# Gated linear attention into a gMLP: a pair of chunks first, decays as one exponential, fewer shifts, another order table

## Chip, cores and metric

The kernel runs on one core of one Trainium2 chip. Its time is device microseconds of one execution. Before the change the median of three runs is 139.16 us (138.14, 139.16 and 139.8).

The engines are named as in the profile: PE (TensorE, matmuls), PEld (its weight loads), DVE (VectorE), ACT (ScalarE), POOL (GpSimd) and SP (SyncE), whose queue issues all large loads and stores.

## The reference

Two parts follow each other. The first is a recurrence with a decay for each token, head and state row; the second is a gated MLP that mixes along the sequence.

```python
for t in range(S):                                   # B, H, S, D = 4, 8, 768, 48
    state = alpha[:, :, t, :, None] * state + np.einsum('bhd,bhe->bhde', k[:, :, t], v[:, :, t])
    y[:, :, t] = np.einsum('bhd,bhde->bhe', q[:, :, t], state)
...
h = np.maximum(x @ w_in, 0.0)                        # x: 4 x 768 x 384, w_in: 384 x 1024
u, v = (h[..., :512], h[..., 512:])
v_n = (v - mean(v)) / np.sqrt(var(v) + 1e-06)
v_s = np.einsum('ts,bsd->btd', w_spatial, v_n) + b_spatial[None, :, None]
return (u * v_s) @ w_out
```

## The kernel before, in words

A batch of 768 tokens is six chunks of 128, so there are 24 chunks, numbered i, and 12 pairs of chunks, numbered j = i // 2. For each chunk the kernel takes the logarithm of alpha (op `ln`), sums it along the tokens with a triangular matmul (`cum`, `half`), and takes exp(-sum) and exp(sum) on ACT (`einv`, `eexp`). The keys are multiplied by the first (`kt`), the queries by the second (`qt`); both are transposed on PE (`tr`, `trk`) and copied back (`ev`, `evs`). Scores (`sc`) are masked on DVE (`m`, `ms`), multiplied by the values and added to the part from the old state (`ya`, `y`), and the result is copied into xT (`xe`). `upd` makes the chunk's k'v, `z` adds the old state, and `S` multiplies by the decay over the chunk, exp of the total sum, which `ebc` puts into a small tile; `sb` copies the state to bf16.

Chunks are handled in three ways. A quad (`four_chunks`, line 653) loads four chunks at four tokens a partition, in runs of 768 bytes; a pair (`pair`, line 428) loads two at two tokens a partition, in runs of 384 bytes; a single (`single`, line 870) loads one chunk in runs of 192 bytes. Lines 92 to 94 say which j are which: a quad starts at j = 0 (chunks 0 to 3 of batch 0) and at j = 3 (batch 1), a pair is j = 2 (chunks 4 and 5), and all the rest are singles. A plain pair or quad (j = 0, 2) sums its tokens by matmul alone, the other multiplies neighbouring alphas first (`pr`). Each of alpha, k, q and v is one DMA for a quad, a pair or a single chunk, into one of three rotating buffers.

The decay: the totals are small matmuls with `la` as weights and `ones_col`, `halves_of` or `quarters_of` as the moving operand (lines 471, 700, 901), one column for a head pair and chunk. Each column holds two heads, one in each half of the partitions, and `ebc` (lines 501, 723, 913) takes the exponential of each half by itself into its column of a tile `bc` or `bcq`, whose other half must stay zero so that heads do not mix. That is two activations for each pair, quad or single, and the tiles are zeroed at the start (lines 296 and 316).

The MLP: `v` and `u` are products of xT with the halves of w_in, `ve` and `ue` their relus. `bn` takes the statistics of v on DVE (lines 1067, 1068), `rs` makes 1/std on ACT (Ln, Exp; lines 1077, 1078), `nm` (line 1082) makes the shift -mean/std of two token tiles on DVE, and `vn` normalises, on DVE from mean and 1/std (line 1096) or on ACT from 1/std and the shift (line 1092). `s` mixes along the sequence, `se` adds the bias, `g` gates, `o` is the last product, `oe` evicts it and `st` stores it.

What runs where and when is written out in a table, PLAN (lines 42 to 88). A word such as `P62@0:512#0` says: engine PE, op number 62, PSUM bank 0, and ahead of it a filler matmul of 512 columns on bank 0 (`warm`, line 239, fp32, issued as two records). `replay` (line 109) emits the ops in that order, so each engine's own order is the table's, and each engine takes its instructions strictly in that order. The letters also choose the engine where an op may run on several: evictions and relus on ACT or DVE, key products on POOL or DVE, casts on POOL, ACT or DVE.

At the start, the table loads the quad (four loads of 768 KB), then the first half of w_in that `v` needs, then the pair, batch 1's quad, the second half of w_in and w_spatial between them. POOL builds the masks and triangles; `causal` (line 350), the pair's mask, stands on POOL between two key products of the quad.

Of the kernel before, what the change touches and what calls it, by code (L numbers as in the profile page):

```python
# [21 lines left out]
class Op:  # L22


    def __init__(self, key, engs, emit, deps, take, pe):
        self.key, self.engs, self.emit, self.take, self.pe = key, engs, emit, take, pe
        self.deps = [d for d in deps if d is not None]
        self.done = False


class Slot:
# [11 lines left out]
D2 D0 D4 D1 G9 G11 G5 G6 D3 S56 S57 S59 S58 A60 S12 S169 S170 A61 S275 S171 D8 P62@0:512#0:512#0:512#0 P66@1 P67 P63  # L43
P70@2 P71 P74@3 P75 A68 A64 D79 G82 P91@4,5 P52@6 A69 A72 A76 G7 A78 A92 A84 A65 G88 G87 A73 A77 D85 D90 D81 D93 D53
D83 D80 P103@6,4,5,7:512#7:424#7 P94@0,1 D86 D104 D89 D106 G13 P97@6,2:192#2 D98 A95 P100@3,0 D101 A96 P117@3,6:376#1
P115@4,1 A99 G107 G14 A15 A173 D102 D109 P128@0,2 D119 D118 P174@5 A116 A122 A176 P130@6,4 S16 D132 D131 S172 A135
P175@1 A129 P120@3 P54@2 G110 G105 P136@0,4 A121 A178 A55 G111 G108 P133@6 G181 A180 A134 G184 A179 D112 A177 D138
P123@7,3 P141@2 S20 G279 G280 G281 G17 G19 G18 D124 D125 P151@6 P187@7,4 P126@3 S23 S277 S276 D185 A152 A127 G186 G183
G113 G114 D182 P190@5,6 A189 A192 A142 P144@3 D137 P139@4 D188 D191 A140 G22 G21 D153 D143 P199@6,5 P196@2,7 P162@4
A283 A145 P290@0 A163 P154@1 P160@3 A282 A291 A155 D200 D201 D198 D197 D164 P193@4 A161 P156@7 A157 A165 D194 D146  # L50
P158@5 A159 G195 P202@1,2 P203 S26 A204 A147 D166 P293@4 P37@5,7 D38 P34@3,6 G24 S278 S387 S399 G25 S506 S29 D35
P207@1 D148 D208 D36 A39 A292 P205 P284@7 P40@3,5 A206 A285 A167 G10 D42 P210@2 D149 D150 D41 S388 S389 D168 D209 S401
S400 P287@5 P223@6 P219@3 P221@1 A211 A294 A224 A288 D212 A286 A220 A213 D298 D304 A289 A295 D214 D222 D215 A216
P225@6 P233@2 P217@3 P229@7 P237@0 A218 A28 D301 G300 G27 D307 G297 P226 D227 G303 G306 P43@3,5 D45 P230 P234 D231
D235 A296 A44 P46@4,6 P309@5,1 D311 P238 P49@7,3 D50 D51 A48 A47 A310 P312@2,6 P318@1,4 P315@5,7 P249@3 P250 A313 A319
A317 A299 A314 A302 D316 D320 D239 G236 D251 P341@4,1 P335@7,5 P245@0 P246 G305 G308 D336 D342 G232 P321@7,6,3,2 G240
G228 D343 D322 A510 G33 D337 D324 D247 P253@4 P333@7,1 P254 P241@5 P242 G323 A391 A403 A30 A340 A334 A32 G325 P392@0
D255 P348@7,6 D243 D327 D350 A393 P344@4 A394 P338@5 G31 G328 D397 D330 D349 G396 P404@3 A345 A339 A405 A406 P257@1
A395 S495 S390 A258 P260@4 P359@2 S402 G407 G248 G326 G329 S494 S560 P346@0,7 D408 P354@3,5 P410@1,6 A360 D331 A347
A353 A411 D356 D355 P362@2 G252 G398 P351@7 A352 P357@3 D412 S508 S497 S509 P421@6,1 P416@5,0 D361 S496 S507 S562 S550  # L60
S548 S611 S561 S551 S549 A358 A363 D418 D423 P511@7 P369@3 P413@0 P374@2 P380@1 D414 D417 A261 A512 P378@0 D422 A498
D364 A375 A564 P263@5 P499@6 G244 G332 G409 G256 A370 A379 A513 D371 G415 A500 A501 P419@0 P424@3 A425 G517 G505 G503
D381 D382 D516 G515 A420 P266@2 P269@4 A502 A365 A383 A270 D366 D504 P429@0 P426@1 P438@3 P440@6 D384 A368 A430 A427
P436@4 A437 A441 A385 D264 D439 P272@0 D367 D267 D428 D431 D386 P521@1 P372@4 A514 A273 P565@6 P376@2 A377 A432 A552
P442@7 A568 P529@0 D443 D522 P456@3 D433 D434 A435 A566 A567 D373 P452@7 P553@1 P518@2,5 A519 A554 A556 D520 A555 P457
D458 D530 D570 G569 G523 G557 G459 P444@4 P445 P448@5 D446 P453 D454 P468@6 P449 D558 D450 P533@7,4 P524@2,0 P572@1,3
D525 G451 G455 P472@5 P469 P460@2 P473 D526 D534 D535 G531 G447 D474 S623 A559 P575@7 D576 A573 P461 S625 S612 S563
A615 D470 D462 P616@4 P527@5 P536@1 A627 S613 A574 P579@7,3 P588@6,0 G577 A617 A528 D589 A618 A537 P628@5 A629 A571
G475 P538@2 A630 P464@1 S624 S614 S730 S718 S721 S626 S720 G620 D621 D581 D580 S733 S732 P476@6 G631 G578 P541@3
P584@7 A539 A619 A542 P465 S784 S719 A477 D632 P634@5,4 D590 A636 D466 D585 S731 A722 P591@3 S786 S772 S785 S773 S835  # L70
S774 A592 S787 S775 G622 G532 P582@1 A583 D635 D540 P637@7 P482@6 A633 A483 P723@5 G586 G471 D638 G639 A724 P645@3,4
P640@0,2 D543 G463 G587 P479@7 P604@6 P596@1 D646 D642 D641 A734 A726 D647 G729 G467 A605 A741 G727 P593@3 P600@6 A594
# [16 lines left out]

PAIRS = (2,)
QUADS = (0,3)
PLAIN = (0, 2)
IDLE = 16

SPLIT = ()
SMALL = ()


SUMS = (
# [30 lines left out]
def kernel(  # L132
# [134 lines left out]
    def op(key, engs, emit, deps=(), take=(), use=(), pe=None):  # L267
# [3 lines left out]
        for s in list(take) + list(use):  # L271
            s.users.append(o)
# [15 lines left out]
    def zeros(n):  # L288
        def emit(_):
            if n == 0:  # L290
# [5 lines left out]
                for t in bcs:  # L296
                    nc.vector.memset(t, 0.0)
# [967 lines left out]
```

## Time and profile before

| what | value |
|---|---|
| three runs | 138.14, 139.16, 139.8 us |
| profiled execution: span, first to last instruction | 137.9 us |
| busy: PE, DVE, ACT, POOL | 130.1, 120.2, 107.7, 86.6 us |
| DMA moved | 28.66 MB, mean 208 GB/s |
| first logarithm on ACT | 5.48 us |
| first product of w_in with xT on PE | 19.71 us |
| first store | after 92 us |

For the profiled execution the page has the span alone. What lies around it is the difference to a run's time: 0.24 us to the shortest run, 1.26 us to the median.

A row by stretches has, after the stretch and its length, the busy us of PE, PEld, DVE, ACT and POOL with the number of instructions in brackets, then the granted PE clock, the mean busy share of the DMA engines and GB/s. A row of the timeline has the start, the length, engine, line, operation, what it writes and reads, how many were merged, and in square brackets the idle time before it and what ended it. A row of a group has the count, the busy time and mean ns of one, then the idle time before them. A row of the waits has who waited for whom, the sum in us, how often, and the longest.

### The profile page before, as it was taken

The page shows a single profiled execution, that of the slowest core. Times are in us where ns is not written, and L with a number is a line of the kernel's source. Part 1 is how long each engine was busy: PE and PEld are TensorE (multiplying, and loading weights), DVE is VectorE, ACT ScalarE, POOL GpSimd, SP SyncE. Part 2 cuts the span into 40 slices and gives each one's busy share as a digit, 9 for nine tenths or more (in the row PEclk, how much of TensorE's full clock was granted, in tenths as well). Part 3 has the DMA queues.
Part 4 walks back from the last instruction along what each step waited for, and adds up shares of the span by engine and source line. Part 5 has one row for each costly group of instructions (what it writes and reads, how often), then busy time and mean ns, then how long its engine had stood idle before and what let it go on. Part 6 is the DMA issues. An engine that isn't in the chain of part 4 may idle for free.

```text
span 137.9 us, 5298 instructions
## 1 busy us (share of the span) xinstructions
PE 130.1 (94%) x2108; PEld 79.4 (58%) x2122; DVE 120.2 (87%) x300; ACT 107.7 (78%) x261; POOL 86.6 (63%) x146
## 2 busy tenths in 40 slices
PE   6999998999999999799999999999999999999990
PEld 3365555565566556466657676656576765566560
DVE  6259999989989999899899999997999999974960
ACT  3476998999999799699997989999865796953040
POOL 7355899993499799761079989520799841004550
PEclk9999999999999999999999999999999999999999
DMA  3999999499989788699999898999960597101064
GB/s 88 370 372 381 344 349 361 106 373 382 355 162 281 159 168 165 124 186 188 193 204 201 164 209 156 189 186 216 213 134 5 187 349 270 63 0 57 0 233 172
DMA packets 76521, 28.66 MB, mean 208 GB/s; under 512 B 63056, under 2 KB 74960, under 8 KB 76496
## 3 DMA queue, kind: packets, MB, share of 16 engines
q1 hardware_dynamic: 76464, 28.32, 77.8%
q8 instruction: 16, 0.26, 0.8%
q14 instruction: 9, 0.07, 0.2%
q0 software_dynamic: 32, 0.00, 0.0%
HBM read 23.60 MB, written 4.72 MB: 205 GB/s over the span
## 4 chain that ended last, share of the span: by engine, by line
PE 60%; DMA 19%; POOL 8%; issue 3%; SPq 3%; ACT 3%; DVE 0%; POOLq 0%; ACTq 0%
PE bank L1005 43%; DMA raw_w<-in_moe_w_spatial_dram 6%; DMA kc<-in_k_dram 5%; DMA raw_w<-in_moe_w_out_dram 4%; DMA ac<-in_alpha_dram 4%; PE bank L960 3%; SPq L883 3%; PE bank L944 2%; PE bank L988 2%; PE bank L416 2%; POOL w_row L180 2%; POOL kt L189 2%; PE bank L932 1%; PE bank L898 1%; POOL state L189 1%
## 5 line engine op out<-in xcount | busy, mean ns | idle before, releaser
L1005 PE MATMUL bank<-w_spT,vn 128*128 128x384 bf16 x192 | 35.6, 327 | 0.0
L189 POOL TENSOR_TENSOR gT<-vs,uT 128x384 bf16<-128x384 f32 x28 | 25.7, 933 | 14.1 <-DVE vs L1152 14.1
L189 POOL TENSOR_TENSOR kt<-kc,binv 128x384 bf16<-128x384 f32 x22 | 20.2, 928 | 22.3 <-ACT binv L908 15.2
L1005 PEld LDWEIGHTS <-vn 128*128 128x128 bf16 x192 | 17.5, 98 | 11.2 <-issue 0.3
L1005 PE MATMUL bank<-w_in,xT 128*128 128x512 bf16 x58 | 17.4, 380 | 1.6 <-ACT xT L178 0.7
L1005 PE MATMUL bank<-xT,w_in 128*128 128x384 bf16 x96 | 18.7, 326 | 0.0
L1005 PE MATMUL bank<-w_out_sb,gT 128*128 128x384 bf16 (+1 forms) x100 | 18.4, 320 | 0.0
L1152 DVE TENSOR_TENSOR vs<-bank,bsp_bc 128x384 f32<-128x384 f32 x31 | 16.3, 549 | 2.4 <-PE bank L1005 2.3
L949 DVE TENSOR_TENSOR ptm<-bank,mask 128x512 bf16<-128x512 f32 x28 | 17.9, 682 | 0.5 <-PE bank L944 0.3
L178 ACT COPY kqT<-bank 128x512 bf16<-128x512 bf16 (+1 forms) x20 | 15.0, 793 | 3.1 <-PE bank L988 1.9
L1067 DVE BATCH_NORM_STATS2 stats<-v_sb 128x6 f32<-128x512 bf16 x24 | 16.4, 683 | 0.6 <-ACT v_sb L184 0.5
L184 ACT ACTIVATE v_sb<-bank 128x512 bf16<-128x512 f32 x20 | 11.7, 597 | 2.0 <-PE bank L1005 1.7
L184 ACT ACTIVATE uT<-bank 128x384 bf16<-128x384 f32 x27 | 12.4, 494 | 0.7 <-PE bank L1005 0.6
L1005 PEld LDWEIGHTS <-w_in 128*128 128x128 bf16 x96 | 9.0, 97 | 6.7 <-DVE ptm L949 0.3
L189 DVE TENSOR_TENSOR qt<-qc,bank 128x384 bf16<-128x384 f32 x24 | 12.6, 545 | 0.2 <-DMA qc<-in_q_dram 0.2
L1005 PEld LDWEIGHTS <-gT 128*128 128x128 bf16 x100 | 9.2, 98 | 5.8
L178 ACT CAST xT<-bank 128x384 bf16<-128x384 f32 x23 | 10.4, 482 | 1.1 <-PE bank L416 0.8
L843 DVE TENSOR_TENSOR ptm<-bank,mask 128x512 bf16<-128x512 f32 x16 | 10.3, 683 | 0.2 <-PE bank L836 0.2
L242 PE MATMUL bank<-junk 128*128 128x512 f32 (+3 forms) x14 | 8.8, 763 | 1.0 <-DVE junk L1231 1.0
L1005 PEld LDWEIGHTS <-xT 128*128 128x128 bf16 x72 | 6.2, 97 | 6.2 <-ACT xT L178 1.2
L178 ACT COPY raw_w<-bank 128x384 f32<-128x384 f32 x8 | 3.8, 479 | 7.3 <-PE bank L1005 7.2
L393 DVE TENSOR_TENSOR zs<-bank,state 128x384 f32<-128x384 f32 x16 | 8.8, 548 | 0.5 <-PE bank L932 0.4
(162 smaller groups left out, 264.3 us busy)
## 6 DMA issues: line engine op xcount, KB each, us to landing
ac<-in_alpha_dram SPq DMA_DIRECT2D x14, 192.0 KB, 4.4
kc<-in_k_dram SPq DMA_DIRECT2D x14, 192.0 KB, 4.4
qc<-in_q_dram SPq DMA_DIRECT2D x14, 192.0 KB, 4.4
vc<-in_v_dram SPq DMA_DIRECT2D x14, 192.0 KB, 4.2
raw_w<-in_moe_w_spatial_dram SPq DMA_DIRECT2D x3, 768.0 KB, 7.8
out_dram<-raw_w SPq DMA_DIRECT2D x11, 192.0 KB, 2.1
out_dram<-o_sb SPq DMA_DIRECT2D x9, 192.0 KB, 2.0
ac<-in_alpha_dram SPq DMA_DIRECT2D x2, 768.0 KB, 6.7
```

The costliest lines, as they stand in the source:

```text
L178: nc.scalar.copy(out=out, in_=in_)
L184: nc.scalar.activation(out=out, in_=in_, func=AF.Relu)
L189: ENG[eng].tensor_tensor(out=out, in0=in0, in1=in1, op=ALU.mult)
L242: nc.tensor.matmul(out=banks[n][:, 0:cols].rearrange("p (a b) -> p a b", a=4), lhsT=junk, rhs=junk[:, None, 0:cols // 4].to_broadcast([128 ...
L393: lambda _: nc.vector.tensor_tensor(out=zs[i % 3], in0=tp(), in1=state[(i - 1) % 3], op=ALU.add),
L843: nc.vector.tensor_tensor(out=ptm[n2][:, ci, s], in0=banks[sl.bank].rearrange("p (hp t) -> p hp t", hp=HP), in1=mask[:, 3][:, None, :].to_ ...
L883: nc.sync.dma_start(out=t[x].rearrange("p hp s d -> p (hp s) d"), in_=src[b, :, c * C:c * C + C, :].rearrange("h s d -> s h d"))
L949: nc.vector.tensor_tensor(out=ptm[n2][:, ci, s], in0=banks[sl_p[s].bank].rearrange("p (hp t) -> p hp t", hp=HP), in1=mask[:, 2][:, None, : ...
L960: nc.tensor.matmul(out=place(to, 3 * hp + (0, 1, 1, 2)[x]), lhsT=heads(vb, hp, x), rhs=ptm[n2][:, ci, x // 2, hp, :], start=(turn == 0), s ...
L1005: nc.tensor.matmul(out=ps, lhsT=lhsT, rhs=rhs, start=first and n == 0, stop=last and n == len(pairs) - 1)
L1067: nc.vector.bn_stats(out=stats[tt % 2], in_=v_sb[n2][:, tt, :])
L1152: nc.vector.tensor_tensor(out=vs[d], in0=banks[sl.bank][:, 0:TH], in1=bsp_bc[:, th, :], op=ALU.add)
```

## The change

Five things are changed together.

1. The chunks of batch 0: a pair is j = 0 (chunks 0 and 1), a quad starts at j = 1 (chunks 2 to 5). Batch 1 keeps its quad at j = 3, and the rest are singles as before. Both of batch 0 stay plain.
2. Decays: a new function `decays` writes, for each head pair and chunk, two columns (one for each half of the partitions). A first small matmul of `own_half` by `off_half` puts -1024 where a half doesn't own the column, the sums are added to it, and one exponential over the whole gives the decay with zeros in the other half. `ebc` is one activation where it was two. `ones_col`, `halves_of` and `quarters_of` have their columns twice; `bc` and `bcq` are not zeroed any more; four more fills make `own_half` and `off_half`.
3. `nm` makes a shift only for a tile that the table normalises on ACT. The table does so for 1 tile of 24; the one before did for 6, and made all 24 shifts.
4. The bias product `bb` waits for the pair's sum `cum 0 1` instead of `cum 1 1`; sums with decays also wait for `zeros 0`.
5. A new order table. On SP the pair's loads come first, alpha of the quad after alpha, k and q of the pair, and both halves of w_in only after all eight loads of batch 0. Ahead of the first sum stand fillers of 512, 512, 512, 512 and 248 columns (before: three of 512); further fillers of 312, 512, 480, 112, 136, 136 and 104 columns follow in batch 0 (before: 512, 424, 192, 376). POOL makes the quad's triangles and `one` at the start, and `causal` after the first key product. Some evictions, casts and products change engines.

```diff
-PAIRS = (2,)
-QUADS = (0,3)
-PLAIN = (0, 2)
+PAIRS = (0,)
+QUADS = (1, 3)
+PLAIN = (0, 1)
...
+FAR = -1024.0
...
-                for t in bcs:
-                    nc.vector.memset(t, 0.0)
+                nc.vector.memset(own_half.bitcast(FP32), 0.0)
+                nc.vector.memset(off_half, 0.0)
+                for s in range(2):
+                    nc.vector.memset(own_half[32 * s:32 * s + 1, 64 * s:64 * s + 64], 1.0)
+                    nc.vector.memset(off_half[32 * s:32 * s + 1, :, 1 - s:2 - s], FAR)
...
+    def decays(cm, n, parts):
+
+        width = 2 * n * HP
+        nc.tensor.matmul(
+            out=cm[:, DM:DM + width], lhsT=own_half, rhs=off_half[:, 0:n * HP, :].rearrange("p a s -> p (a s)"),
+            start=True, stop=False)
+        of = ones_col if n == 1 else (halves_of if n == 2 else quarters_of).rearrange("p c s -> p (c s)")
+        for hp in range(HP):
+            for x, la in enumerate(parts):
+                nc.tensor.matmul(
+                    out=cm[:, DM + 2 * n * hp:DM + 2 * n * hp + 2 * n], lhsT=la[:, hp].rearrange("p s d -> p (s d)"),
+                    rhs=of, start=False, stop=(hp == HP - 1 and x == len(parts) - 1))
...
-            for s in range(2):
-                nc.scalar.activation(out=bc[half(s), :, :, s], in_=tot_view()[half(s)], func=AF.Exp)
+            nc.scalar.activation(
+                out=bc.rearrange("p hp c s -> p (hp c s)"), in_=banks[sl_c[3].bank][:, DM:DM + 8 * HP], func=AF.Exp)
...
             for x in (tt - 1, tt):
+                if engine_of[made[("vn", b, x)].n] != "ACT":
+                    continue
                 nc.vector.tensor_scalar(
...
-        made[("bb", th)].deps.append(made[("cum", 1, 1)])
+        made[("bb", th)].deps.append(made[("cum", 0, 1)])
```

The order tables, cut to their beginnings:

```diff
-D2 D0 D4 D1 G9 G11 G5 G6 D3 S56 S57 S59 S58 A60 S12 S169 S170 A61 S275 S171 D8 P62@0:512#0:512#0:512#0 P66@1 P67 P63
...
+G9 D4 S56 D0 A60 G5 G6 G8 P61@0:512#0:512#0:512#0:512#0:248#0 A63 P62@1 G11 D3 P52@2 G10 D1 D2 S57 A65 G71 D68
...
```

More of the change, by code (lines that the diff above doesn't have):

```diff
@@ L48 @@
[L48 to L52, printed above, removed]
@@ L899, in cum @@
             if not last:
-                for hp in range(HP):
-                    nc.tensor.matmul(
-                        out=cm[:, DM + hp:DM + hp + 1], lhsT=la[:, hp].rearrange("p s d -> p (s d)"), rhs=ones_col,
-                        start=True, stop=True)
-        op(("cums", i), "PE", cum, [("lns", i), ("one",), ("zeros", 2)], take=[sl_c],
-           pe=(0.0, 384, 0, 2) if last else (0.241, 1, 0, 10))
+                decays(cm, 1, [la])
+        op(("cums", i), "PE", cum, [("lns", i), ("one",), ("zeros", 2), ("zeros", 0)], take=[sl_c],
+           pe=(0.0, 384, 0, 2) if last else (0.262, 2, 0, 12))
         buf = binv[i % 4].rearrange("p (hp s) d -> p hp s d", s=2)
```

144 lines of the change are left out of this document (68 added, 76 removed).

## The prediction, made blind

> **What bounds the kernel now.** I read the page first, then busy time by stretches, then the timeline of the start, then the groups of instructions, then the waits.
>
> ```profile
> span 137.9 us, 5298 instructions
> PE 130.1 (94%) x2108; PEld 79.4 (58%) x2122; DVE 120.2 (87%) x300; ACT 107.7 (78%) x261; POOL 86.6 (63%) x146
> ```
>
> The share over the span says TensorE. By stretches (columns: PE, PEld, DVE, ACT, POOL, clock, DMA) it is finer:
>
> ```profile
> 14.00:16.00 2.00, 2.00 (x59) 1.23 (x58) 1.98 (x6) 2.00 (x5) 1.50 (x3) 1.00 1.16 338
> 24.00:26.00 2.00, 1.77 (x48) 1.13 (x40) 1.86 (x5) 1.94 (x5) 2.00 (x6) 1.00 0.24 83
> 46.00:50.00 4.00, 3.98 (x74) 2.55 (x72) 4.00 (x9) 3.59 (x11) 3.31 (x6) 1.00 0.80 157
> 58.00:62.00 4.00, 3.10 (x68) 2.05 (x69) 3.22 (x9) 3.88 (x14) 2.06 (x4) 1.00 0.98 191
> 70.00:80.00 10.00, 9.95 (x159) 6.50 (x159) 9.84 (x20) 8.59 (x20) 9.43 (x13) 1.00 0.96 191
> 120.00:130.00 10.00, 10.00 (x62) 5.82 (x61) 7.00 (x18) 3.52 (x9) 2.35 (x3) 1.00 0.05 20
> ```
>
> From 14 us to about 118 us TensorE and VectorE are both full to a few per cent; only after 118 us is TensorE alone. A microsecond taken from one of the two is therefore worth a microsecond only where the other can follow. The start is the one stretch that neither fills with real work:
>
> ```profile
> 1.05 5.49 PE L242 MATMUL bank<-junk 128*128 128x512 f32 x6 [1.05 <-DVE junk L1231]
> 5.48 1.58 ACT L682 ACTIVATE la<-ac 128x768 bf16<-128x768 f32 x2 [3.47 <-DMA ac<-in_alpha_dram]
> 6.37 0.39 PE L717 MATMUL bank<-la,le_quad 128*128 128x384 bf16 x1
> 7.11 0.81 PE L717 MATMUL bank<-la,lt_quad 128*128 128x384 bf16 x4
> 8.20 0.91 POOL L189 TENSOR_TENSOR kt<-kc,binv 128x384 bf16<-128x384 f32 x1 [3.46 <-ACT binv L740]
> 8.53 1.55 DVE L189 TENSOR_TENSOR kt<-kc,binv 128x384 bf16<-128x384 f32 x2 [3.74 <-ACT binv L740]
> 9.07 1.90 POOL L354 TENSOR_SCALAR_AFFINE_SELECT mask<-mask 64x128 bf16<-64x128 bf16 x4
> 10.18 1.84 PE L242 MATMUL bank<-junk 128*128 128x512 f32 x4
> 13.78 0.61 POOL L180 CAST w_in<-raw_w 128x512 bf16<-128x512 f32 x1 [1.37 <-DMA raw_w<-in_moe_w_in_dram]
> ```
>
> TensorE does filler until 6.37 us, VectorE has no data until 8.53 us.
>
> **The change part by part.**
>
> *Engine moves and fewer shifts.* I counted both order tables by kind and engine. VectorE loses 23 of 24 shifts (only one normalisation stays on ScalarE), and one triangle copy group, two output copies, two relus of v, two v casts, one transposed copy of 1024, one product with the decay and three smaller copies; it gains five normalisations, five relus of u, four xT copies, two transposed copies of 512, one cast of w_out and one key product. The larger rows:
>
> ```profile
> L1084 DVE TENSOR_SCALAR shift<-mvs,rstd 128x1 f32<-128x1 f32 x24 | 3.9, 204 | 1.2 <-ACT rstd L1078 1.2
> L1096 DVE TENSOR_SCALAR vn<-v_sb,mvs,rstd 128x512 bf16<-128x512 bf16 x18 | 6.9, 404 | 0.0
> L186 DVE TENSOR_SCALAR uT<-bank 128x384 bf16<-128x384 f32 x5 | 2.8, 552 | 0.3 <-PE bank L1005 0.3
> L1092 ACT ACTIVATE vn<-v_sb,shift,rstd 128x512 bf16<-128x512 bf16 x6 | 4.9, 815 | 0.2 <-DVE shift L1084 0.2
> L178 ACT CAST xT<-bank 128x384 bf16<-128x384 f32 x23 | 10.4, 482 | 1.1 <-PE bank L416 0.8
> L184 ACT ACTIVATE uT<-bank 128x384 bf16<-128x384 f32 x27 | 12.4, 494 | 0.7 <-PE bank L1005 0.6
> ```
>
> Shifts: 23 x 3.9/24 = -3.7 us. Gains: 5 x 0.404 + 5 x 0.552 = +4.8 us; four xT copies at the 0.52 that such an eviction takes, +2.1. The rest, at the means of their groups, is -4.4. Net on VectorE: -1.3 us. It is full, so I book all of it: -1.3 (bounds 0, if TensorE holds it back, and -3.7, if only the shifts count). ScalarE: five normalisations -4.1, five relus -2.5, four xT copies -1.9, against some +6.3 of other copies and casts that come to it: -2.2 us before the next part.
>
> *One decay exponential a chunk.*
>
> ```profile
> L915 ACT ACTIVATE bc<-bank 64x4 f32<-64x4 f32 x22 | 3.7, 169 | 0.6 <-DVE qt L189 0.3
> L725 ACT ACTIVATE bcq<-bank 64x16 f32<-64x16 f32 x4 | 0.7, 176 | 0.0
> L504 ACT ACTIVATE bc<-bank 64x8 f32<-64x8 f32 x2 | 0.4, 178 | 0.0
> 9.05 0.54 PE L700 MATMUL bank<-quarters_of,la 128*128 128x4 bf16 x16
> L901 PE MATMUL bank<-ones_col,la 128*128 128x1 bf16 x44 | 2.7, 165 | 0.0
> ```
>
> 28 activations become 14: 4.8/2 = -2.4 us on ScalarE, so -4.6 in all there. TensorE gets 14 more matmuls (the -1024 that wipes the foreign half). Sixteen small ones took 0.54 us with 0.165 for the last to come out: 25 ns each beyond the first. Bounds 14 x 0.025 = 0.35 and 14 x 0.165 = 2.3; each also has weights of its own, so I take +0.5, nearer the first, since they stand in a row of their like. The zero fills of the decay tiles fall away and as many fills of own_half and off_half come: they lie before 5 us, when VectorE waits for data until 8.53, and cost nothing.
>
> What is ScalarE's -4.6 worth? It is seldom what ends an idle stretch of TensorE:
>
> ```profile
> PE bank L960 <- ACT uT L184: 1.0, 1, 1.0
> PE bank L1005 <- ACT xT L178: 0.7, 2, 0.5
> PE bank L1005 <- ACT rstd L1078: 0.2, 1, 0.2
> PE bank L1005 <- ACT sbd L178: 0.2, 1, 0.2
> ```
>
> 2.1 us in all. Bounds 0 and -2.1; I take half, -1.0, because the 1.0 us wait at 58 us falls where a load was late as well, and is as likely to stay.
>
> *The start.* The pair's alpha is 384 KB instead of 768, in as many pieces. At the rates of these rows
>
> ```profile
> 4.00:6.00 2.00, 2.00 (x3) 0.59 (x3) 0.57 (x6) 0.52 (x1) 0.61 (x4) 1.00 1.09 372
> 6.00:8.00 2.00, 2.00 (x11) 0.96 (x10) 0.00 (x0) 1.43 (x3) 0.00 (x0) 1.00 1.10 368
> ```
>
> 768 KB take 2.1 us, and 384 KB at the 338 of 14 to 16 us (where the pair's loads ran) 1.2 us, so the logarithm could begin near 4.8 instead of 5.48 and end at 5.7. But ahead of the first cumulative sum the new table has filler of 4 x 512 + 248 columns where 3 x 512 stood. Six records took 5.49 us; two more of 512 and two of 248 follow. At 10.18 us, 512 and 424 columns twice took 1.84, half as long a column. The clock has doubled by 7.1, where four sums take 0.81 (0.33 and three steps of 0.16). If it doubles near 6, the filler ends at about 7.4: the first sum is 1.0 us later than 6.37, not earlier. Ends: 5.8 (only the logarithm counts) and 8.7 (all at the slow rate).
>
> [...]
>
> ```profile
> 9.63 0.49 ACT L740 ACTIVATE binv<-bank 128x384 bf16<-128x384 f32 x1 [0.35 <-PE bank L700]
> 11.81 1.48 DVE L189 TENSOR_TENSOR qt<-qc,bank 128x384 bf16<-128x384 f32 x3 [0.21 <-DMA qc<-in_q_dram]
> 14.66 1.08 DVE L180 COPY kqT<-bank 128x512 bf16<-128x512 bf16 x3
> 16.24 2.53 DVE L843 TENSOR_TENSOR ptm<-bank,mask 128x512 bf16<-128x512 f32 x4
> ```
>
> From 7.4 on by rows: two sums and decays to 8.7; first exp(-sum) 8.0 to 8.5; key product on VectorE 8.5 to 9.3, so it starts when it does now. The second key product goes to POOL at 9.3 (its decays come first) and the causal mask now stands behind it instead of between two key products, which takes 1.9 us off a path; the other masks moved ahead (triq, one: some 2 us) end before 7 and are hidden by the wait until 8.2 now. Then VectorE waits for exp (0.5), for the transposes (0.1) and for the first scores (0.8; filler of 312, 512 and 480 columns stands in front): 1.45 us of gaps with a pair alone, where VectorE now has the second half's key product, casts and be to do and loses the 0.21 of the row above. I take +1.2 (bounds -0.6, the start at 5.8 with its gaps covered, and +2.5, the start at 8.7).
>
> *The queue of loads.* On SP four loads of a quad stand ahead of w_in now, and its cast begins at 13.78. The four of the pair come ahead of it too: 1.57 MB at 338 GB/s, 4.7 us, so 18.4. Its readers are held anyway: TensorE's order has the output of chunk 2 ahead of the first v, and VectorE's work up to its masks is two key products 1.6, six query products 3.0, seven transposed copies 2.6, six masks 3.8, one decay product and two state sums 1.7, an xT copy 0.5: 8.5 + 13.2 + 1.45 = 23.1 us. So the queue costs nothing beyond the start's term; without that cover up to 4.7. What now starts first of that kind:
>
> ```profile
> 19.71 1.57 PE L1005 MATMUL bank<-w_in,xT 128*128 128x512 bf16 x5
> ```
>
> That becomes some 3.4 us later, and four v, twelve matmuls at about 0.2, 2.5 us of TensorE's work, are then still to do that are done by 25 us now; I book nothing for them, since VectorE and not TensorE is the fuller there (row of 24 to 26), and some can go into later idle time, as the 0.9 us of 58 to 62.
>
> *Sum*: +1.2 (start) -1.3 (VectorE) +0.5 (matmuls) -1.0 (ScalarE) = -0.6. Against the profiled 137.9 of span that is 137.3. The median of the runs, 139.16, is 1.26 above this span; with the same distance: 138.6 us.
>
> **The rivals.**
>
> *All relief, no ramp (faster).* Start term 0, VectorE -1.3, ScalarE the full -2.1, matmuls +0.35: -3.0, 136.1; with half of the start's term 136.8. For it: both full engines lose work, and the mask leaves the path. Against it: two full engines must both gain.
>
> *TensorE starved until w_in's turn (slower).* The first v at 23.1 instead of 19.7, the 2.5 us of deferred work not regained, since from 70 to 80 us TensorE idles 0.05 us only; matmuls +0.5 to +0.9, VectorE's relief worthless because TensorE holds it back: +3.0 to +3.4, 142.2; with part regained 141.5. It decides if the first v comes after 23.5 us and TensorE's idle time between 30 and 62 does not shrink. Against it: VectorE, not TensorE, is full between 14 and 58.
>
> *The clock stays low through the filler.* First sum at 8.7, start term +2.5: 138.6 + 1.3 = 139.9, and more if the sums after it run slowly too. Against it: in the profiled run it had doubled before 7.1 us, with less filler. [...]
>
> *The earlier pair does nothing*: it is the forecast's own start term, the filler holding the first sum whatever alpha does.
>
> **How the numbers follow.** About 1% (1.4 us) is what a measurement of this kernel can tell from no change; the three runs spread over 1.7 us. Forecast 0.37 (its own range 137.6 to 140.0), relief 0.33, starvation 0.20, slow clock 0.10. Faster by over 1% (below 137.8): 0.33 + 0.02 = 0.35. Slower (above 140.5): 0.20 + half of 0.10 + 0.03 = 0.28. Within: 0.37. The range of 8 in 10 runs from 136.6, which leaves out the fuller end of the relief, to 141.0, which leaves out most of the starvation.
>
> **What the new profile would show.** Right: the first sum between 7 and 8 us, the first key product at about 8.5, the first v near 23; VectorE's busy time near 119 and ScalarE's near 103; decay exponentials 14; idle TensorE between 24 and 62 smaller. Wrong: a first sum near 6 or 9; decay groups that cost over 1 us more on TensorE; a VectorE with gaps between 24 and 60, which would mean that another engine or a load took over as the bound.

## The result, and the profile after

The changed kernel takes 151.4 us (median of four runs, 150.75 to 152.63) where the kernel before takes 139.11 beside it: a ratio of 1.0915 (1.084 to 1.0991). The forecast was 138.6, the range ended at 141.0. Ratios leave out runs more than 1.5% above the fastest of their kernel, medians do not. In the changed kernel the granted clock differs from run to run (means of 0.949 to 0.966); where that decides, runs are set side by side by their spans and the time that each spent at half clock, which is twice the span times what its mean clock lacks of 1.

The profiled execution took 150.75 us. The page of the changed kernel, its filler group, and the filler group of the kernel before:

```profile
span 148.7 us, 5292 instructions
PE 136.6 (92%) x2127; PEld 82.7 (56%) x2138; DVE 120.2 (81%) x278; ACT 103.7 (70%) x244; POOL 85.1 (57%) x148
PEclk9999996559999999999999999999999999999999
...
L246 PE MATMUL bank<-junk 128*128 128x512 f32 (+6 forms) x24 | 12.2, 638 | 1.7 <-DVE quarters_of L323 1.0 <-ACT kqT L180 0.7
```

```profile
L242 PE MATMUL bank<-junk 128*128 128x512 f32 (+3 forms) x14 | 8.8, 763 | 1.0 <-DVE junk L1231 1.0
```

These rows split the 10.8 us of span (148.7 - 137.9) by what TensorE does. Filler: 12.2 - 8.8 = 3.4. Other products: 124.4 - 121.3 = 3.1, though only 14 small ones were added; PEclk gives the likely reason, it reads 6, 5 and 5 in three slices of 3.7 us. Idle: 12.1 - 7.8 = 4.3. The ends of matmuls are modelled, so each of the three is rough.

Nearly all of it is lost early. The first 32 us as one stretch (columns as before), first the kernel before, then the changed one, each followed by the same stretch for the filler alone:

```profile
0.00:32.00 32.00, 29.59 (x565) 16.57 (x570) 25.77 (x86) 24.91 (x57) 24.92 (x51) 1.00 0.94 306
0.00:32.00 32.00, 8.82 (x14) 3.13 (x14) 0.17 (x1) 1.00 0.94 306
```

```profile
0.00:32.00 32.00, 26.45 (x410) 15.41 (x412) 17.50 (x59) 16.66 (x35) 18.08 (x49) 0.87 0.84 237
0.00:32.00 32.00, 12.19 (x24) 5.42 (x24) 0.17 (x1) 0.87 0.84 237
```

TensorE has 20.8 us of real work behind it in the one and 14.3 in the other, part of that at half clock; VectorE is 8.3 us behind. From 32 us on both kernels are about equally full: before, 100.5 us of other products in the 105.9 that remain; after, 110.2 in 116.7, which is 1.1 us more of idle time. So the cause is to be sought ahead of 32 us.

The timeline of the changed kernel there (ScalarE's first logarithm, then TensorE, then VectorE's first key product):

```profile
4.44 0.84 ACT L469 ACTIVATE la<-ac 128x768 bf16<-128x768 f32 x1 [2.43 <-DMA ac<-in_alpha_dram]
...
7.71 0.33 PE L487 MATMUL bank<-la,le_pair 128*128 128x384 bf16 x1
...
11.15 0.32 PE L1036 MATMUL bank<-b_sp_sb,ones_row 1*128 1x384 bf16 x1 [2.42 <-DMA b_sp_sb<-in_moe_b_spatial_dram]
11.39 1.65 PE L246 MATMUL bank<-junk 128*128 128x512 f32 x4
12.98 0.41 PE L549 MATMUL bank<-ident,kt 64*128 64x64 bf16 x16
...
31.10 0.61 PE L1009 MATMUL bank<-w_in,xT 128*128 128x512 bf16 x1
...
8.76 0.56 DVE L191 TENSOR_TENSOR kt<-kc,binv 128x384 bf16<-128x384 f32 x1 [4.69 <-ACT binv L510]
```

Up to 8.8 us the forecast holds (first sum 7.4 foreseen, key product 8.5). Then TensorE stands until 11.15 for a load of 1.5 KB. The chain of waits names it, and what it stands behind on GpSimd:

```profile
5.12 0.11 POOL lt_quad L341
...
5.33 5.77 DMA b_sp_sb<-in_moe_b_spatial_dram
...
11.15 0.32 PE bank L1036
11.46 1.58 PE bank L246 x4
```

In the kernel before, the same load and its first reader, which has no idle time before it:

```profile
2.31 0.67 POOL L1195 DMA_DIRECT2D b_sp_sb<-in_moe_b_spatial_dram  x1
...
9.92 0.33 PE L1032 MATMUL bank<-b_sp_sb,ones_row 1*128 1x384 bf16 x1
```

The bias load is issued at 5.33 because the table now has GpSimd build the pair's triangles, the identity and the quad's triangles ahead of it (2.42 to 5.39 us), and lands 5.8 us later. `bb`, which reads it, is the third op of TensorE's order; the key transposes and a filler of 1.65 us stand behind it. The first product of w_in comes at 31.10 us, against 19.71 before and 23.1 in the forecast.

### The profile page after: what moved, and what is told of

Its sections match the earlier page's. It is cut to its first block, busy times and chain, and to the rows that moved or that the text cites. A ratio compares the mean times of both kernels' runs of the same rounds, so it can differ in the third digit from the quotient of the medians.

```text
span 148.7 us, 5292 instructions
## 1 busy us (share of the span) xinstructions
PE 136.6 (92%) x2127; PEld 82.7 (56%) x2138; DVE 120.2 (81%) x278; ACT 103.7 (70%) x244; POOL 85.1 (57%) x148
## 2 busy tenths in 40 slices
DMA packets 76519, 28.64 MB, mean 193 GB/s; under 512 B 63056, under 2 KB 74960, under 8 KB 76496
## 4 chain that ended last, share of the span: by engine, by line
PE 73%; DMA 7%; DVE 6%; POOL 4%; ACT 4%; issue 3%; SPq 0%; POOLq 0%; ACTq 0%; DVEq 0%
PE bank L1009 46%; DMA b_sp_sb<-in_moe_b_spatial_dram 4%; PE bank L246 3%; DMA out_dram<-o_sb 3%; PE bank L947 3%; PE bank L992 2%; PE bank L964 2%; PE bank L776 2%; PE bank L841 2%; PE bank L437 2%; PE bank L904 2%; DVE vn L1102 2%; PE bank L799 1%; PE bank L935 1%; POOL kt L191 1%
## 5 line engine op out<-in xcount | busy, mean ns | idle before, releaser
L191 POOL TENSOR_TENSOR kt<-kc,binv 128x384 bf16<-128x384 f32 x21 | 19.4, 931 | 16.5 <-ACT bank L748 5.2
L1009 PEld LDWEIGHTS <-vn 128*128 128x128 bf16 x192 | 17.5, 97 | 12.9 <-issue 2.1
L180 ACT COPY kqT<-bank 128x1024 bf16<-128x1024 bf16 (+1 forms) x19 | 15.0, 814 | 7.6 <-PE bank L549 3.4
L1009 PE MATMUL bank<-xT,w_in 128*128 128x384 bf16 x96 | 19.4, 326 | 0.0
L1009 PE MATMUL bank<-w_in,xT 128*128 128x512 bf16 x61 | 18.5, 400 | 1.0 <-issue 0.4
L186 ACT ACTIVATE v_sb<-bank 128x512 bf16<-128x512 f32 x22 | 13.0, 601 | 2.2 <-PE bank L1009 2.2
L246 PE MATMUL bank<-junk 128*128 128x512 f32 (+6 forms) x24 | 12.2, 638 | 1.7 <-DVE quarters_of L323 1.0
L849 DVE TENSOR_TENSOR ptm<-bank,mask 128x512 bf16<-128x512 f32 x16 | 10.4, 683 | 2.3 <-PE bank L841 2.2
L186 ACT ACTIVATE uT<-bank 128x384 bf16<-128x384 f32 x22 | 10.1, 495 | 2.1 <-PE bank L1009 2.1
L180 ACT CAST xT<-bank 128x384 bf16<-128x384 f32 x19 | 8.7, 482 | 2.6 <-PE bank L437 2.4
L246 PEld LDWEIGHTS bank<-junk 128*128 128x128 f32 x24 | 5.4, 254 | 9.1 <-issue 6.7
L182 DVE COPY kqT<-bank 128x512 bf16<-128x512 bf16 (+1 forms) x15 | 6.7, 487 | 4.6 <-PE bank L549 2.8
```

What stands on the lines that cost most here:

```text
L180: nc.scalar.copy(out=out, in_=in_)
L182: ENG[eng].tensor_copy(out=out, in_=in_)
L186: nc.scalar.activation(out=out, in_=in_, func=AF.Relu)
L191: ENG[eng].tensor_tensor(out=out, in0=in0, in1=in1, op=ALU.mult)
L246: nc.tensor.matmul(out=banks[n][:, 0:cols].rearrange("p (a b) -> p a b", a=4), lhsT=junk, rhs=junk[:, None, 0:cols // 4].to_broadcast([128 ...
L849: nc.vector.tensor_tensor(out=ptm[n2][:, ci, s], in0=banks[sl.bank].rearrange("p (hp t) -> p hp t", hp=HP), in1=mask[:, 3][:, None, :].to_ ...
```

## The experiments

| run | what differs | us, median (lowest to highest) | ratio to the kernel before |
|---|---|---|---|
| e1_bias_first | after, bias load issued first | 147.57 (146.33 to 149.43) | 1.07 (1.0623 to 1.0777) |
| e2_no_later_filler | after, no filler behind the first | 147.45 (146.38 to 148.2) | 1.0641 (1.0586 to 1.0696) |
| e3_before_decays | before, new decays | 141.06 (140.77 to 141.12) | 1.0181 (1.0156 to 1.0207) |
| e4_before_fewer_shifts | before, 18 shifts less | 138.34 (138.09 to 138.66) | 0.9985 (0.9962 to 1.0007) |
| e5_before_pad | before, 320 unused bytes | 141.18 (141.1 to 141.59) | 1.0183 (1.0141 to 1.0226) |
| e6_before_decays_aligned | e3, 192 unused bytes | 138.53 (138.28 to 139.38) | 1.0005 (0.9977 to 1.0033) |
| e7_after_aligned | after, 192 unused bytes | 146.11 (144.48 to 146.39) | 1.0508 (1.0436 to 1.058) |
| e8_after_aligned_bias_first | e7 and e1 | 146.31 (144.43 to 148.24) | 1.0448 (1.0372 to 1.0525) |
| e9_no_later_filler | e8, no filler behind the first | 144.8 (143.58 to 145.55) | 1.0455 (1.039 to 1.052) |
| e10_early_w_in | e8, w_in's first half ahead of the quad's v | 149.71 (148.33 to 150.5) | 1.082 (1.0734 to 1.0907) |
| e11_short_first_filler | e9, first filler as before | 144.48 (143.98 to 145.25) | 1.0446 (1.0396 to 1.0495) |
| e12_filler_in_the_waits | e8, filler where TensorE waits | 144.65 (144.19 to 147.5) | 1.0442 (1.0399 to 1.0484) |
| e13_quad_half_kqv | e12, 1.18 MB less to load | 143.0 (142.63 to 144.5) | 1.0331 (1.0273 to 1.039) |
| e14_quad_half_all | e12, 1.57 MB less to load | 142.74 (141.99 to 143.8) | 1.0274 (1.0218 to 1.0331) |
| e15_before_pair_loads_first | before, the pair's loads first | 145.51 (144.41 to 145.71) | 1.0476 (1.0423 to 1.0528) |
| e16_before_decays_shifts_aligned | e6 and e4 | 138.93 (138.41 to 141.36) | 1.0026 (0.9996 to 1.0056) |
| e17_half_kqv_no_later_filler | e13, no filler behind the first | 144.77 (143.69 to 146.08) | 1.0419 (1.034 to 1.0498) |
| e18_half_kqv_before_filler | e17, first filler as before | 143.63 (142.86 to 144.09) | 1.0357 (1.0312 to 1.0403) |

The kernel before took 138.28 to 138.6 us beside them.

### The bias load, the fillers, and two parts on the table of before

e1: the op moves to the second place of GpSimd's order, where it stood before the change.

```diff
-G9 D4 S56 D0 A60 G5 G6 G8 P61@0:512#0:512#0:512#0:512#0:248#0 A63 P62@1 G11 D3 P52@2
+G9 G11 D4 S56 D0 A60 G5 G6 G8 P61@0:512#0:512#0:512#0:512#0:248#0 A63 P62@1 D3 P52@2
```

> The changed kernel with one word of its table moved: POOL issues the load of the bias ahead of the triangles, at about 2.4 us instead of 5.33. Theory 1 (a wait sets it off: the bias product stands third on TensorE and holds it from 8.65 to 11.15): the wait of 2.4 us is gone, the first transposes stand near 10.6 instead of 12.98, everything up to the first product with w_in (31.1 us) comes at least 2.4 us earlier, and more if the clock no longer falls: 143 to 149 us. Theory 2 (w_in is late behind eight loads): the first product with w_in stays near 31 and the time near 151. Theory 3 (the pair's ramp leaves TensorE so empty that its clock is halved whatever the bias does): 149, with some 10 us at clock 0.5 still there.

e2: the seven fillers behind the first sum go, from six words of the table, as in

```diff
-P74@3,4:512#3:312#3
+P74@3,4
```

> The changed kernel without the seven fillers behind the first sums (512, 312, 480, 112, 136, 136, 104 columns); the five ahead of them stay. Theory 1: the fillers were planned for idle time, but behind the late bias product they stand on the path, 1.65 + 1.07 + 0.47 + 0.59 + 0.82 + 0.76 = 5.4 us of busy time, of which the chain shows about 5: 146 to 148. Theory 3: without them TensorE is emptier, the clock falls earlier or for longer and eats the gain: 151 to 154.

e3 has the table, the chunks and all the shifts of before, with the function `decays`. e4 is the kernel before, with the shift left out for tiles that VectorE normalises.

> The kernel before with its own order table and chunks, and only the decays changed (one exponential, one more small matmul for each sum, other zero fills). By the terms of the prediction: matmuls +0.35 to +0.5, ScalarE relief 0 to -1.0 of its 2.4 us: 138.5 to 139.5. If the new decays are themselves dear (the 14 matmuls with weights of their own at 0.165 each and more, or sums that wait for them): 140.5 and above.

> The kernel before with its own table, where a shift is made only for the six tiles that ScalarE normalises: 18 of 24 small VectorE instructions less, 2.9 us of its busy time. If VectorE's time passes on to the end: up to -1.5, 137.6 to 138.6. If TensorE holds VectorE back: no difference, 139.1.

Each of the first two takes 4 us off, by their medians, and brings the first product of w_in from 31.10 to 27.14 and 28.64 us. In e1 the clock moves along: its runs have 3.4 to 13.9 us at half clock, those of the changed kernel 10.1 to 15.2. At like half clock (147.4 us of span with 13.9, against 149.3 to 149.6 with 15) the bias load is worth some 2 us. In e2 the clock moves little: three of its four runs have 14 us at half clock and take 145.5 to 146.3, so behind the late bias load the seven fillers cost some 3.5 us. e4 is no change, though its 18 shifts less take 2.0 us off VectorE's busy time (120.2 to 118.2); this part of VectorE's relief is worth nothing. e3 is the surprise: 14 small matmuls and half the exponentials cost 2.6 us. The loads give it away. From 4 to 12 us, first the kernel before, then e3:

```profile
4.00:12.00 8.00, 8.00 (x60) 3.73 (x63) 3.83 (x13) 5.57 (x13) 4.18 (x11) 1.00 1.09 376
```

```profile
4.00:12.00 8.00, 6.95 (x57) 3.48 (x56) 3.74 (x14) 5.45 (x13) 4.08 (x10) 1.00 1.11 330
```

Same loads, DMA engines as busy (1.09 and 1.11), 12% fewer bytes.

### Where the load buffers stand

`own_half` and `off_half` are 256 and 64 bytes a partition. With them every tile allocated later begins 320 bytes higher, the buffers of the loads too, which began at multiples of 512 bytes. e5 adds nothing but 320 unused bytes to the kernel before; e6 and e7 add 192 to e3 and to the changed kernel, which makes 512 with the 320.

```diff
     halves_of = consts.tile([128, 2], BF16, name="halves_of")
+    pad = consts.tile([128, 160], BF16, name="pad")
```

> The kernel before with one unused tile of 320 bytes behind halves_of, so that every tile behind it, the load buffers among them, stands 320 bytes higher, as in the changed kernel; no instruction differs. Placement theory (writes of loads that don't start at a multiple of 256 bytes in the partition cost more): the 384-byte packets go from 22.4 ns to about 27, the loads of 4 to 12 us to 320 to 345 GB/s, and the time from 138.5 to between 140.0 and 141.2 us, the 2.6 us of e3_before_decays. Rival (the loads in e3 were slower because other work, the new decay products, ran beside them): no change, 138.2 to 138.8 us, packets as before.

> e3_before_decays with an unused tile of 192 bytes behind off_half, so that the load buffers stand at multiples of 512 bytes again. Placement theory: packets of 22.4 ns and 137.9 to 138.9 us, against 141.06 in e3. Rival (the decays over both halves cost the 2.6 us themselves): 140.6 to 141.3 us.

> The changed kernel with the same 192 unused bytes; nothing else differs. Placement theory: the same 2 to 3 us come back, 148 to 149.5 us against 151.4. Rival (TensorE waits for the bias load at 11.15 us and the loads have slack behind it): 150.5 to 151.6 us.

The stretch from 4 to 12 us of e5, e6, the changed kernel and e7:

```profile
4.00:12.00 8.00, 7.88 (x56) 3.66 (x55) 3.74 (x12) 5.51 (x13) 4.14 (x11) 1.00 1.11 330
```

```profile
4.00:12.00 8.00, 6.88 (x59) 3.41 (x59) 3.83 (x15) 5.53 (x13) 4.17 (x11) 1.00 1.10 376
```

```profile
4.00:12.00 8.00, 5.58 (x23) 2.67 (x23) 1.65 (x4) 2.58 (x5) 5.14 (x18) 1.00 1.19 292
```

```profile
4.00:12.00 8.00, 5.77 (x25) 2.65 (x24) 1.65 (x4) 2.58 (x5) 5.69 (x19) 0.97 1.13 352
```

The rate falls and returns with the place alone, and so does the time: 2.7 us by unused bytes, and all of e3's loss back. Mean ns of a packet, worked out from the DMA records of the traces:

```
packet      before   e3     e5     e6     after   e7
192 B       15.6    15.5   15.6   15.5   15.7    15.5
384 B       22.4    27.4   27.3   22.5   27.1    22.7
768 B       36.9    40.6   41.1   36.8   41.1    36.6
2048 B      86.6    92.4   92.9   87.2   89.7    84.6
```

With the buffers 320 bytes higher the packets of 384, 768 and 2048 bytes take longer (e5 against the kernel before: +22%, +11%, +7%), and with 192 more they are back (e6); those of 192 bytes show nothing. The theory ahead of e5 puts the bound at multiples of 256 bytes; that doesn't come out. A pair's runs of 384 bytes lie one behind the other, so in the kernel before they begin 0, 384, 256 and 128 bytes behind a multiple of 512 in turn, and 99% of them take 22 ns all the same. So what is shown is the price of these 320 bytes; why they cost it, and which other shifts would, no run shows.

These runs also settle the decays: aligned, they cost nothing and bring nothing (1.0005, to 0.4 us either way), and neither do decays and shifts together (e16). So -1.0 for ScalarE and +0.5 for the matmuls were together worth nothing measurable; no run has the one without the other.

> The parts of the change other than its order, on the table of before: one exponential a chunk for the decays, shifts for the six tiles that ScalarE normalises alone, and 192 unused bytes that put the load buffers back on multiples of 512. If what the prediction booked for ScalarE were worth something here, 137.2 to 138.0; if nothing, 138.0 to 138.6, as the kernel before.

### Bias, filler and clock with the loads in place

> e1_bias_first with the 192 unused bytes. If placement and the bias load add up: 147.6 less 2.6, 144.0 to 145.6 us, with the first product of w_in at about 25 us and 5 to 7 us over the kernel before still to be explained. If both hide in the same wait: 147 to 148 us.

e8 didn't beat e7 by its median, and in the profiled runs its first product of w_in stands at 28.2 us (e7: 28.4), not at the 25 expected. The runs of each, by span (what lies around the span differs, by 1.9 to 3.5 us in e8), show what hides it: e7 144.4 and 143.9 us with 3.5 us at half clock each, 142.5 and 143.4 with none; e8 144.7 and 145.3 with 10.1 and 10.2, 142.5 and 143.4 with 3.4. At like half clock (3.4 to 3.5) the early bias load is worth 1.2 us, from two runs on each side that differ by up to 0.9 among themselves. Within e8, 6.75 us more at half clock cost 2.05, 0.3 us for each; in the same way the runs of e7 give 0.3, those of e1 0.4 and those of the changed kernel 0.15.

What the clock fell behind is seen in stretches cut at its own steps (PE alone, then clock, DMA share, GB/s). Changed kernel, e8, kernel before:

```profile
16.76:20.18 3.42, 3.13 (x103) 1.00 1.07 365
20.18:23.59 3.41, 1.84 (x52) 1.00 1.06 359
23.59:27.00 3.41, 3.41 (x78) 0.50 0.54 129
27.00:30.42 3.42, 3.42 (x66) 0.50 0.02 7
30.42:33.83 3.41, 3.19 (x22) 0.50 0.95 249
```

```profile
12.50:15.92 3.42, 3.42 (x49) 1.00 1.10 378
15.92:19.33 3.41, 2.13 (x99) 1.00 1.04 401
19.33:22.74 3.41, 3.41 (x73) 0.50 1.02 316
```

```profile
20.20:23.61 3.41, 2.94 (x72) 1.00 1.08 364
23.61:27.03 3.42, 3.19 (x74) 1.00 0.48 120
```

Here a step of 3.41 us with 1.84 or 2.13 us of work is followed by half clock, one with 2.94 is not. The bound is not sharp: in the changed kernel two earlier steps (6.5 to 13.35 us) have 2.20 each and keep the clock, while e2 and e11 lose it behind steps with 2.5. Half clock then stays for one to three steps, though TensorE is busy in them by the records (3.41, 3.42 and 3.19 us of each in the changed kernel). The traces have falls of two kinds: in e8's step of 2.13 us the longest gap is 0.7 us, while ahead of e7's fall TensorE stands for 2.23 us in one piece, at the late bias load. Why the clock falls, no run shows.

Now the fillers. e9 removes the seven again; e11 was to shorten the first alone, but what ran has none of the seven either, so it stands beside e9; e12 lengthens one and adds one where TensorE waits anyway:

```diff
-P147@1,7 P150@5,1:112#1
+P147@1,7:220#1 P150@5,1:300#5
```

> e8_after_aligned_bias_first without the seven later fillers (312, 512, 480, 112, 136, 136, 104 columns). Theory fillers: in e8 they stand on the path from 8.6 to 26 us for 5.2 us, of which their readers' other waits take part back: 140.5 to 142.5 us, first product of w_in 3 to 4 us earlier than e8's 28.2. Theory order (the quad's key products, its loads and its copies are late anyway, and the filler only fills the wait): 143.5 to 146 us, with the wait of TensorE for other engines longer by what the filler took; and the clock lower for longer.

> e8_after_aligned_bias_first with three fillers of 512 columns ahead of the first sum, as before the change, where it has 4 x 512 + 248. The prediction's start term: first sum near 6.2 instead of 7.8 us, and 1.0 to 1.6 us off the time if the path goes through it, 143 to 145. Rival (the next filler, 512 + 312, and the quad's alpha hold what follows): 144.4 to 146.5, no change.

> e8_after_aligned_bias_first with a filler of 220 columns ahead of the quad's first key transposes, where TensorE waits 0.4 us for GpSimd, and 300 columns on a free bank where 112 wait for a copy. Clock theory (3.4 us with over 1 us of idle TensorE are followed by half clock): the idle time of 16 to 19 us goes from 1.3 to about 0.3 us, the clock stays whole and the time is 142 to 143.5 us, or the fall comes a step later and the time is 143 to 145. Rival (the half clock costs little, since other engines hold this stretch): clock whole, time as in e8, 144.4 to 146.5.

The filler groups of e9 and e12:

```profile
L247 PE MATMUL bank<-junk 128*128 128x512 f32 (+1 forms) x10 | 5.5, 712 | 1.0 <-DVE quarters_of L324 1.0
```

```profile
L248 PE MATMUL bank<-junk 128*128 128x512 f32 (+7 forms) x26 | 11.2, 548 | 1.0 <-DVE quarters_of L325 1.0
```

All three come out at 144.5 to 144.8, in different ways. e9 executes 5.5 us of filler where e8 has 12.0, and spends 10 to 12 us of every run at half clock; beside e8's two runs with 10 us at half clock it takes 2.2 us less (142.8 and 145.0 of span, means). e11 against e9 says that 512 + 248 columns less ahead of the first sum are worth nothing here; it has 10 to 14 us at half clock. e12 keeps the clock for all but 0 to 5.2 us and pays 11.2 us of filler. Filler and half clock are two prices of one thing: there is too little real work on TensorE at this place. In all three the first product of w_in stands at 26.1 to 26.3 us.

### The queue of loads

> e8_after_aligned_bias_first with the first 768 KB of w_in ahead of the quad's values on the queue of loads, its three casts on ScalarE behind the first xT copy, and the first two v products in place of the fillers of 112 and 136 columns. The prediction's rival, TensorE starved until w_in's turn: the first product of w_in at 19 to 21 us, and 142.0 to 143.5 us against 144.4 to 146.5. Rival (what is late is the chain of the quad's state, which w_in doesn't feed): 144 to 146.5 us though the first product comes 7 us earlier.

e10 brings the first product of w_in to 19.89 us, as early as before the change, and loses 3.4 us by the medians, more than either expectation allowed. The quad's values are then late, and ScalarE, which now casts w_in (17.38 to 19.04 us) in front of the quad's copies, holds those up too. What VectorE waits for; the second row is the wait for the first exponential, which every kernel here has:

```profile
DVE zs L415 <- PE bank L820: 4.3, 1, 4.3
DVE kt L191 <- ACT binv L511: 3.5, 1, 3.5
DVE kqT L182 <- PE bank L777: 3.0, 1, 3.0
```

So w_in's turn by itself is not what starved TensorE; what the quad needs has to come first. e13 and e14 take bytes out of the quad's loads and leave every instruction behind them. They, and e17 and e18 after them, leave heads 4 to 7 of chunks 2 to 5 out of the computation; constants stand in their place.

```diff
+                hs = 4 if j == 1 and x in ('kc', 'qc', 'vc') else 8
+                if hs == 4:
+                    nc.vector.memset(t[x][:, 4:8].rearrange("p h a d -> p (h a d)"), 1.0 if x == "ac" else 0.0)
                 nc.sync.dma_start(
-                    out=t[x].rearrange("p h a d -> p h (a d)"),
-                    in_=src[b, :, t0:t0 + 4 * C, :].rearrange("h (p a) d -> p h (a d)", a=4))
+                    out=t[x][:, 0:hs].rearrange("p h a d -> p h (a d)"),
+                    in_=src[b, 0:hs, t0:t0 + 4 * C, :].rearrange("h (p a) d -> p h (a d)", a=4))
```

> e12_filler_in_the_waits, with the first quad's keys, queries and values loaded for four of the eight heads; the other four are filled with zeros at the start, so heads 4 to 7 of chunks 2 to 5 are left out of the computation. Every instruction behind stays. That takes 1.18 MB, 3.1 us at some 370 GB/s, out of the queue ahead of the quad's values and of w_in. Theory queue (the 1.57 MB of the pair, put ahead of the quad, hold everything behind the pair's own work): first product of w_in at about 23.2 instead of 26.3 us and 141 to 142.5 us, against 144.65. Rival chain (the quad's sums, key products and copies follow each other engine by engine, and the loads have landed by then): 144 to 145 us, first product after 25.8.

> As e13_quad_half_kqv, and alpha too for four heads (ones in the others): 1.57 MB less in all, as much as the pair's four loads put ahead of the quad. Theory queue: 4.2 us off the arrival of the quad's values, first product of w_in at about 22 us, 139.8 to 141.5 us, that is most of the 6 us by which e12_filler_in_the_waits is behind the kernel before. Rival chain: 144 to 145 us, as in e12.

> The kernel before with nothing changed but the place of the pair's four loads (chunks 4 and 5) on SP: ahead of the quad's instead of behind them. The price of the queue without the pair's work ahead: the quad's alpha comes 4.2 us later and the whole start with it, 142 to 143 us. If the start had slack in it, under 140.5.

First e12, then e13: the first product of w_in and the first 32 us.

```profile
26.25 2.27 PE L1011 MATMUL bank<-w_in,xT 128*128 128x512 bf16 x6
```

```profile
0.00:32.00 32.00, 28.89 (x518) 16.50 (x519) 21.31 (x67) 20.79 (x43) 22.49 (x54) 0.95 0.89 286
```

```profile
24.13 1.47 PE L1014 MATMUL bank<-w_in,xT 128*128 128x512 bf16 x5
```

```profile
0.00:32.00 32.00, 30.33 (x532) 17.36 (x536) 25.55 (x75) 23.36 (x50) 23.69 (x55) 1.00 0.81 261
```

The queue is on the path: 3.1 us of loads are worth 2.1 us of the first product and 1.65 us of the time (144.65 to 143.0), or 1.4 where the clock is whole (142.5 and 141.1 us of span). Both fall short of what the theory gave, the product at 23.2 us and a time of 141 to 142.5. (Of VectorE's 4.2 us more, 2.8 are the zero fills, by its busy time on the two pages, 123.7 and 120.9.) But it is not all: another 0.39 MB, alpha's half, bring 0.3 by the medians, less than the runs of either kernel differ among themselves (e14, whose profiled run has its first sum late, at 8.02, and its first product of w_in at 25.03), and 4.2 us stay. e15 prices the queue where no work of the pair stands ahead: the first sum goes from 6.37 to 11.40 us, TensorE waits 5.7 us for the logarithm, the clock is halved for some 8 us, and the time is 6.9 us longer.

Is the rest filler?

> e13_quad_half_kqv (heads 4 to 7 of chunks 2 to 5 left out of the computation) without any filler behind the one ahead of the first sum. Theory filler: what e13 is still behind the kernel before, 4.4 us, is TensorE's time for 11.4 us of filler against 8.8, so 5.9 us of filler less give 139 to 141 us as long as the clock stays whole. Rival (the order of the later work, which fillers don't touch): 142.5 to 144 us. If the clock falls to a half for 7 us, about 2 us more in both.

> e17_half_kqv_no_later_filler with the filler ahead of the first sum as before the change, 3 x 512 columns instead of 4 x 512 + 248. Theory filler: first sum 0.5 to 1.0 us earlier and 0.5 to 1.0 us less than e17. Rival: as e17.

No, or not by itself: without the later filler e13 gets 1.8 us slower, with 10.4 to 11.1 us at half clock in each run, and e18 wins back 1.1 of it by the medians, their ranges overlapping. That theory fell. What holds VectorE in e17, after the wait for its first exponential, are TensorE's results and copies, one after the other:

```profile
DVE ptm L853 <- PE bank L845: 1.9, 2, 1.5
DVE zs L415 <- PE bank L803: 1.0, 1, 1.0
DVE ptm L602 <- POOL vb L182: 0.8, 1, 0.8
DVE kqT L182 <- PE bank L780: 0.7, 1, 0.7
```

In the kernel before, the waits of VectorE from 7 to 32 us are 3.7 us for its first exponential and then 0.6 us in all:

```profile
DVE kt L189 <- ACT binv L740: 3.7, 1, 3.7
DVE w_spT L180 <- ACT rstd L1077: 0.4, 1, 0.4
DVE qt L189 <- DMA qc<-in_q_dram: 0.2, 1, 0.2
```

That a pair followed by a quad gives a thinner chain than a quad followed by a pair is what these rows suggest for the last 4 us; no run here shows it by itself, and which link would have to be shortened stays open. Of the 3.3 us of span by which the profiled e13 is behind (141.2 and 137.9), 1.8 are products that it hasn't done by 32 us, with 2.6 us more filler in their place (30.3 - 11.4 against 29.6 - 8.8), and the rest is idle time behind. Of the kernels with the new order that compute everything none comes within 4% of the kernel before.

## Why the prediction was wrong

Its sum was -0.6 on the span; +10.8 was measured. By its steps:

- *The start, +1.2.* Right to 8.8 us, with luck in the first sum: the forecast let the fillers double their speed near 6 us, the author's estimate, and in this profile they did at about 6.5 (from one record of 512 columns in 0.85 us to one in 0.43). With the same five fillers they did so anywhere from 3.9 to 7.1 us in the other kernels' profiles, and the first sum stood at 6.41 (e9) to 8.02 (e14), where the forecast had 7 to 8 as its sign of being right. The granted clock reads 1 all through this, so the half clock counted above leaves the start out. The step fails at "the other masks moved ahead (triq, one: some 2 us) end before 7 and are hidden by the wait until 8.2". The builds are hidden; what stood behind them on GpSimd's queue was not asked. The bias load is 3.0 us later than before (issued at 5.33 instead of 2.31), its reader stands ahead of the key transposes on TensorE, and 2.4 us of idle time follow. Its price at like clock is 1.2 us (e8) or, with the load buffers 320 bytes higher, some 2 (e1); by e1's median, in which the clock moves along, it is 3.8.
- *The fillers behind the first.* The text allowed 0.8 us for the first scores and let the wait cover 312, 512 and 480 columns. Once the chain is late, filler is on it: the seven cost some 3.5 us behind the late bias load (e2) and 2.2 at like clock in e8 (against e9). With the bias load early they couldn't be dropped for a gain of that size either: the clock then falls (e9, e17).
- *The queue, "costs nothing beyond the start's term; without that cover up to 4.7".* The cover was VectorE's own work, which was to reach to 23.1 us. VectorE had 17.5 us of work in 32 where it had 25.8. Measured: 1.65 us for 3.1 us of loads (1.4 at whole clock), and 1.9 for 4.2.
- *The fills of own_half and off_half, "cost nothing".* Their time does cost nothing, their 320 bytes cost 2.7 us on the table of before (e5). On the changed table e7 gets 5.3 back, of which at 0.3 us each the shorter half clock (0 to 3.5 us instead of 10 to 15) is some 3.
- *VectorE -1.3, ScalarE -1.0, matmuls +0.5.* VectorE's busy time didn't fall (120.2 in both; 18 shifts are 2.0 us of it in e4, where their group's mean gave 2.9), ScalarE's did as foreseen (103.7 for 103, 14 exponentials). What was run alone moved nothing: shifts (e4), decays (e6), both (e16); the moves between engines were not run alone. The relief was booked against stretches that look full on two engines. By e4 VectorE does not set the end; from 32 us on TensorE is the fuller one before the change (100.5 us of 105.9, VectorE 94.4).
- *The rivals.* "Starved until w_in's turn" had the right direction, and half of its mark came true (first v after 23.5 us). The other half did not: TensorE's idle time between 30 and 62 shrank, from 1.45 to 0.60 us. It gave 142.2, for a cause that is not enough by e10. "The clock stays low" was weighed for the first 8 us alone; it fell at 23.6 instead, behind a step with 1.6 us of idle time. One of the forecast's own signs of being wrong came true: from 24 to 60 us VectorE is idle for 5.4 us, in the kernel before for 2.1.

The parts overlap, since the clock fell behind a wait or in one (of 2.23 us in e7, 5.7 in e15), so they add up only roughly to the 12.3 us between the medians (12.9 against the 138.46 measured beside e1): placement 2.7, bias 1.2 to 2, half clock some 3 to 4.5 at 0.3 us each, queue 1.4 to 1.9, and some 4 us of filler and thinner chain that no run separates.

## What to carry to other kernels

When an order table changes, follow every op that moved on every queue to its first reader, the 1.5 KB loads too: one such load held TensorE for 2.4 us. A new constant is an edit to the placement of all that is allocated after it, so compare the addresses of the load buffers, and pad: 320 bytes cost 2.7 us here (e5). When the clock differs between runs, compare runs of like clock before a gain is put down to an edit. Before counting a relief of a full engine, find the one that sets the end by taking work from the other alone: 18 shifts less on VectorE were worth nothing.

## What the runs showed of the hardware that was not expected

- Loads into buffers moved 320 bytes up from multiples of 512 took 27 instead of 22 ns for a packet of 384 bytes and 41 instead of 37 for 768 (e5 and the kernel before); 192 bytes are untouched (15.6 in both), and in the kernel before runs of 384 bytes take 22 ns whether they begin 0, 128, 256 or 384 bytes behind a multiple of 512. By rate it is 330 against 376 GB/s from 4 to 12 us.
- The granted clock fell behind 3.41 us steps in which TensorE was busy for 1.84 us (changed kernel), 2.13 (e8) or 2.5 (e2, e11), with no gap over 0.8 us, and stayed whole behind others with 2.20 (changed kernel) and 2.18 (e1). It stayed at half for three steps with 3.41, 3.42 and 3.19 us of work (changed kernel). Half clock cost some 0.3 us for each microsecond (0.15 to 0.4 between runs of one kernel).
- A load of 1.5 KB issued by GpSimd beside the large loads took 5.8 us to land; in other kernels 5.4 (before), 4.7 (e7) and 3.4 (e8).
